# Three g tiles moved within the on-chip memory of a fused attention and two-MLP kernel

## The chip, the cores and the metric

The kernel runs on one core of a Trainium2 chip. The metric is the device time in microseconds (us) of one execution. Before the change three executions took 1518.82, 1520.11 and 1520.95 us; the median is 1520.11 us.

## The reference

Three stages follow each other. `attention`: q, k and v have 8 batches, 8 heads, 576 positions and 64 columns each; every block of 64 positions attends to itself alone (scores times 1/8, softmax, times v). Its result, seen as x of 4608 tokens by 512, goes through two MLPs:

```python
h = x @ w_in                                   # 512 -> 2048
g = np.maximum(h, 0.0) + np.log1p(np.exp(-np.abs(h)))
x = g @ w_out                                  # 2048 -> 512
h = np.maximum(np.maximum(x @ w1, x @ w2), x @ w3)   # 512 -> 768
out = h @ w_out2                               # 768 -> 512
```

The inputs come as float64 and are rebuilt as pairs of float32 numbers on the chip; all results are float32.

## The kernel before

**Tiling.** Tokens are cut into nine blocks of 512 (b), the hidden width of the first MLP into sixteen strips of 128 (j). Each operand of a matrix product is a tile of 128 partitions by 2 by 512 numbers in float32r: the first half holds the rounded values, the second what rounding left. A product is made in three passes (line 26, `PASS`): high times high, high times low, low times high. So each matmul of TensorE has a moving operand of 512 (or 256) columns, and a stationary operand of 128 columns that a weight load brings in before it. One matmul, one weight load.

**The lines.** `mlp1` holds the first MLP. Line 746 is its first product: 12 matmuls per block and strip, weights and x both in slots, into a `ph` bank. ScalarE takes softplus out of it (line 756), `cut_up` splits the result into a g tile (line 252 writes the high half, line 259 the low half), and line 766 is the second product: 12 matmuls, in which the g tile is the moving operand and a slot holds the weights. In the second MLP line 916 makes the products (moving 256 columns, all operands in slots). `mlp2_out`, line 1034, makes the last product, in which the g tile is the stationary operand and a slot is the moving one. Lines 670 and 723 are the two products of the attention of later blocks, each a batch of 12 and 24 matmuls (moving 256 and 128 columns, all in slots). Line 723 takes its weights 64 columns at a time and its moving operand in pieces of 32 numbers (128 bytes) that lie apart.

**The order.** Each step is an operation with a cost and a due time in a plan (`Plan.order`, lines 102 to 175); the plan simulates the engines with these costs, picks the order and hands out the places. It sees names and counts of places and no address. So two layouts with the same lists of places give the same instructions on every engine, in the same order, with the same waits.

**The layout.** A tile gets its address when it is first made: tiles stand in the order in which they are made, each rounded up to 32 bytes per partition. A partition holds 229,376 bytes; the last slot ends at 229,152. The first tiles are `ident`, `drop` (the offset column, 4 bytes), `mx` (four tiles of 32 bytes for maxima and sums), `rq` (2048 bytes), then the three g tiles (4096 bytes each), nine `tmp`, `rk`, `rv`, `p`, and behind them 46 slots of 4096 bytes (`s` in the profile). A slot takes weights, x, loaded pieces or parts of q, k and v in turn. 4096 and 2048 are multiples of 512, so in the kernel before rq, g, tmp and every slot start at 288 over a multiple of 512 bytes. Every operand of lines 746, 766, 916, 1034 and 670 starts at a multiple of 512 bytes from the start of its tile, so it too starts at 288.

Of the kernel before, what the change touches and what calls it, by code (L numbers as in the profile page):

```python
# [10 lines left out]
F32 = mybir.dt.float32  # L11
F32R = mybir.dt.float32r
# [8 lines left out]
P = 128  # L21
# [157 lines left out]
def tile_kernel(ctx: ExitStack, tc: tile.TileContext, q, k, v, w_in, w_out, w1, w2, w3, wo2, out):  # L179
    nc = tc.nc  # L180
    B, H, S, D = q.shape
# [8 lines left out]
    TB = 512  # L190
# [5 lines left out]
    pool = ctx.enter_context(tc.tile_pool(name="sb", bufs=1))  # L196
# [5 lines left out]
    def mem(kind, n, shape, dt, where=pool):  # L202
        return [where.tile(shape, dt, name=f"{kind}{i}") for i in range(n)]

    ident = pool.tile([P, P], F32, name="ident")
    drop = pool.tile([P, 1], F32, name="drop")
    small = {"mx": mem("mx", 4, [P, H], F32), "rq": mem("rq", 1, [P, TB], F32)}

    places = {

# [5 lines left out]
        "load": list(range(3)),  # L216
        "load0": list(range(4)),
        "pair": list(range(2)),
        "g": mem("g", 3, [P, 2, TB], F32R),
        "tmp": mem("tmp", 9, [P, TB], F32),  # L220
        "rk": mem("rk", 1, [P, TB], F32),
        "rv": mem("rv", 1, [P, TB], F32),
# [943 lines left out]
```

## Time and profile before

| | us |
|---|---|
| median of three executions | 1520.11 |
| the profiled execution | 1520.93 |
| its span, first to last instruction | 1519.1 |
| TensorE busy (PE) | 1499.5 |
| weight loads busy (PEld) | 1317.1 |
| VectorE busy (DVE) | 968.2 |
| ScalarE busy (ACT) | 592.5 |

The profiled execution took 1.8 us more than its span. In the profile PE is a matmul and PEld the weight load that may run beside one. Busy time of a group of matmuls counts each to its modelled end, past the start of the next; the distance from the first start of one batch to that of the next is the measure of what a batch takes. `g<-tmp,g` reads: written tile, arrow, read tiles.

### The profile page before, as it was taken

Reading aid. Unit: us, or ns where it says so; the run is one execution under the profiler, and the core shown is the slowest. Engines: PE = TensorE matmul, PEld = TensorE weight load, DVE = VectorE, ACT = ScalarE, POOL = GpSimd, SP = SyncE. Lnnn points to the kernel's source line nnn. Section 1 sums busy time; section 2 is a strip of 40 time slices with the busy share of each in tenths; the row PEclk is TensorE's granted clock in tenths of the full one; section 3 lists DMA queues with packets and bytes.
Section 4 is the critical chain, followed back from the end, with each engine's and each line's share of the span. In section 5 each row is a group of like instructions: output and inputs, shape, how many; then the busy total and the mean of one; then the engine's idle time right before and its main releaser. Section 6 shows DMA issues by size and latency. Waiting matters only on the chain.

```text
span 1519.1 us, 23062 instructions
## 1 busy us (share of the span) xinstructions
PE 1499.5 (99%) x8930; PEld 1317.1 (87%) x8930; DVE 968.2 (64%) x1841; ACT 592.5 (39%) x1123; POOL 4.6 (0%) x11
## 2 busy tenths in 40 slices
PE   6999999999999999999999999999999999999998
PEld 5787888888888888888888888999999999999997
DVE  7988877867776767767677465554544535445443
ACT  5754344443444343443343344432322323223221
POOL 0000000000000000000000000000000000000000
PEclk9999999999999999999999999999999999999999
DMA  9354233543434325244342221222322222222222
GB/s 257 118 141 129 63 89 98 148 113 77 139 90 109 98 58 146 70 101 101 77 120 81 71 92 54 78 70 84 112 69 85 84 77 105 84 84 76 78 70 84
DMA packets 235214, 147.29 MB, mean 97 GB/s; under 512 B 167008, under 2 KB 202848, under 8 KB 235104
## 3 DMA queue, kind: packets, MB, share of 16 engines
q1 hardware_dynamic: 231904, 144.24, 33.2%
q10 hardware_dynamic: 3200, 1.57, 0.5%
q8 instruction: 70, 1.15, 0.3%
q14 instruction: 40, 0.33, 0.1%
HBM read 109.58 MB, written 36.18 MB: 96 GB/s over the span
## 4 chain that ended last, share of the span: by engine, by line
PE 97%; ACT 1%; DMA 1%; DVE 0%; issue 0%; ACTq 0%
PE acc L766 26%; PE ph L746 26%; PE ph L916 15%; PE one L916 12%; PE acc L1034 10%; PE aps L723 3%; PE aps L670 3%; PE acc L609 1%; PE ph L372 1%; PE acc L560 1%; ACT s L252 1%; DMA s<-in_v_dram 1%; PE acc L529 0%; PE ph L371 0%; DMA s<-wo2d 0%
## 5 line engine op out<-in xcount | busy, mean ns | idle before, releaser
L746 PE MATMUL ph<-s,s 128*128 128x512 f32 x1728 | 416.5, 390 | 1.2 <-DVE s L259 0.9
L766 PE MATMUL acc<-g,s 128*128 128x512 f32 x1728 | 415.3, 390 | 0.0
L766 PEld LDWEIGHTS acc<-g,s 128*128 128x128 f32 x1728 | 322.9, 188 | 67.2 <-issue 1.0
L746 PEld LDWEIGHTS ph<-s,s 128*128 128x128 f32 x1728 | 321.5, 188 | 67.8 <-DVE s L259 1.2
L916 PE MATMUL ph<-s,s 128*128 128x256 f32 x1944 | 267.8, 283 | 0.0
L259 DVE TENSOR_TENSOR tmp<-one,tmp 128x256 f32<-128x256 f32 x241 | 101.9, 423 | 246.9 <-PE one L916 213.1
L916 PEld LDWEIGHTS ph<-s,s 128*128 128x128 f32 x1944 | 251.8, 192 | 4.1
L252 ACT COPY tmp<-ph 128x256 f32<-128x256 f32 x268 | 100.0, 373 | 347.7 <-PE ph L916 346.5
L259 DVE TENSOR_TENSOR g<-tmp,g 128x512 fp32r<-128x512 f32 x198 | 136.2, 688 | 146.3 <-ACT g L252 145.5
L756 ACT ACTIVATE tmp<-ph 128x512 f32<-128x512 f32 x144 | 86.2, 598 | 305.4 <-PE ph L746 302.7
L916 PE MATMUL one<-s,s 128*128 128x256 f32 x1458 | 201.6, 283 | 0.0
L916 PEld LDWEIGHTS one<-s,s 128*128 128x128 f32 x1458 | 186.7, 192 | 0.2
L259 DVE TENSOR_TENSOR s<-tmp,s 64x512 fp32r<-64x512 f32 (+1 forms) x212 | 142.3, 675 | 24.9 <-ACT s L252 21.0
L1034 PE MATMUL acc<-s,g 128*128 128x512 f32 x648 | 157.1, 391 | 0.5 <-DMA s<-wo2d 0.5
L252 ACT CAST s<-tmp 128x512 fp32r<-128x512 f32 (+2 forms) x190 | 115.2, 610 | 60.4 <-DVE tmp L641 26.6
L1034 PEld LDWEIGHTS acc<-s,g 128*128 128x128 f32 x648 | 118.3, 188 | 23.3 <-DMA s<-wo2d 0.9
L252 ACT CAST g<-tmp 128x512 fp32r<-128x512 f32 x192 | 119.4, 622 | 25.6 <-PE acc L766 16.4
L259 DVE TENSOR_TENSOR tmp<-tmp,tmp 128x256 f32<-128x256 f32 (+1 forms) x152 | 83.0, 547 | 3.9
L252 ACT COPY p<-aps 64x512 f32<-64x512 f32 x50 | 29.1, 583 | 66.9 <-PE aps L670 65.7
L252 ACT COPY tmp<-acc 128x512 f32<-128x512 f32 (+1 forms) x66 | 37.3, 588 | 33.4 <-PE acc L1034 15.8
L723 PEld LDWEIGHTS aps<-s,s 128*64 128x64 f32 x672 | 44.5, 135 | 3.7 <-DVE s L259 0.2
L670 PEld LDWEIGHTS aps<-s,s 128*128 128x128 f32 x336 | 44.0, 191 | 2.2
(97 smaller groups left out, 953.8 us busy)
## 6 DMA issues: line engine op xcount, KB each, us to landing
s<-wo2d SPq DMA_DIRECT2D x54, 512.0 KB, 3.3
s<-in_moe_w_out_dram SPq DMA_DIRECT2D x22, 512.0 KB, 4.8
x2d<-tmp SPq DMA_DIRECT2D x36, 256.0 KB, 2.9
s<-in_moe_w_dram SPq DMA_DIRECT2D x18, 512.0 KB, 4.1
s<-x2d SPq DMA_DIRECT2D x18, 512.0 KB, 4.6
s<-in_moe_w_in_dram SPq DMA_DIRECT2D x16, 512.0 KB, 4.9
out_dram<-tmp SPq DMA_DIRECT2D x29, 256.0 KB, 4.5
pd<-tmp SPq DMA_DIRECT2D x28, 256.0 KB, 2.2
```

Of the source, the lines that this page charges most:

```text
L252: nc.scalar.copy(dst(), src())
L259: return op({"D": 0.69 * n}, lambda e: nc.vector.tensor_tensor(dst(), a(), b(), f), r=r, w=w, **kw)
L372: nc.tensor.matmul(o, ident, a.t, start=False, stop=False)
L560: nc.tensor.matmul(o[:, h], qT()[:, h * P:(h + 1) * P], blk[0]()[:, 2 * h:2 * h + 2].rearrange("p u e s -> p (u e s)"), start=True, stop=True,
L609: nc.tensor.matmul(o[:CH, c], rv()[:, c * CH:(c + 1) * CH], blk[1]()[:, c].rearrange("p e s -> p (e s)"), start=True, stop=True,)
L670: nc.tensor.matmul(o[:, h], Qh.t[:, l, h * P:(h + 1) * P], kb[m].t[:, 2 * h * P:2 * (h + 1) * P], start=(n == 0), stop=(n == 2),)
L723: nc.tensor.matmul(o[:CH, c], Vh.t[:, l, c * CH:(c + 1) * CH], z[m][:, c % 2, c // 4, c // 2 % 2], start=(n == 0), stop=(n == 2),)
L746: nc.tensor.matmul(ph.t, w[:, wi, kk * P:(kk + 1) * P], x[kk].t[:, xi], start=(kk == 0 and wi == 0 and xi == 0), stop=(kk == KD - 1 and wi ...
L756: in_line("y", op({"A": 0.6}, lambda e: nc.scalar.activation(l.t, ph.t, AF.Softplus), r=[ph], w=[l], alloc=[l]))
L766: nc.tensor.matmul(acc[m // 2].t[:, m % 2], w[:, wi, m * P:(m + 1) * P], g.t[:, gi, :], start=(first and wi == 0 and gi == 0), stop=(last ...
L916: nc.tensor.matmul(dst(), ws.t[:, wi, col + kk * P:col + (kk + 1) * P], x.t[:, xi, kk * HT:(kk + 1) * HT], start=(first and kk == 0 and wi ...
L1034: nc.tensor.matmul(acc[t // 2].t[:, t % 2], g.t[:, gi, t * P:(t + 1) * P], wo.t[:, wi], start=(j == 0 and wi == 0 and gi == 0), stop=(j == ...
```

## The change

The order in which the small tiles are made is another one. `rq` and the first g tile are made ahead of `mx`, `drop` stands between the second and the third g tile, and two new tiles that nothing reads or writes (32 and 64 bytes) stand ahead of and behind the third g tile. The lists that the plan gets have the same length and order. The addresses, in bytes from the start of a partition:

| tile | before | by 512 | after | by 512 | by 64 (before, after) | slots minus tile, by 512, after |
|---|---|---|---|---|---|---|
| rq | 1824 | 288 | 1664 | 128 | 32, 0 | 256 |
| first g | 3872 | 288 | 3712 | 128 | 32, 0 | 256 |
| second g | 7968 | 288 | 7936 | 256 | 32, 0 | 128 |
| third g | 12064 | 288 | 12096 | 320 | 32, 0 | 64 |
| first tmp | 16160 | 288 | 16256 | 384 | 32, 0 | 0 |
| first slot | 40736 | 288 | 40832 | 384 | 32, 0 | 0 |

Before, the last column is 0 for all. Counted the other way, tile minus slots, the three g tiles are at 256, 384 and 448. The last slot ends at 229,248.

```diff
     ident = pool.tile([P, P], F32, name="ident")
+    small = {"rq": mem("rq", 1, [P, TB], F32), "g": mem("g", 1, [P, 2, TB], F32R)}
+    small["mx"] = mem("mx", 4, [P, H], F32)
+    small["g"].append(pool.tile([P, 2, TB], F32R, name="g1"))
     drop = pool.tile([P, 1], F32, name="drop")
-    small = {"mx": mem("mx", 4, [P, H], F32), "rq": mem("rq", 1, [P, TB], F32)}
+    pool.tile([P, 8], F32, name="apart0")
+    small["g"].append(pool.tile([P, 2, TB], F32R, name="g2"))
+    pool.tile([P, 16], F32, name="apart1")
...
         "pair": list(range(2)),
-        "g": mem("g", 3, [P, 2, TB], F32R),
         "tmp": mem("tmp", 9, [P, TB], F32),
```

## Rows read from the trace of the kernel before

**Rows 1.** The page: busy time, share of the span, instructions; granted clock by slices.
```profile
span 1519.1 us, 23062 instructions
...
PE 1499.5 (99%) x8930; PEld 1317.1 (87%) x8930; DVE 968.2 (64%) x1841; ACT 592.5 (39%) x1123; POOL 4.6 (0%) x11
...
PEclk9999999999999999999999999999999999999999
```

**Rows 2.** The page: the chain that ended last, shares by engine.
```profile
PE 97%; ACT 1%; DMA 1%; DVE 0%; issue 0%; ACTq 0%
```

**Rows 3.** Busy time by stretch, then granted clock, DMA share, GB/s.
```profile
400.00:935.00 535.00, 535.00 (x2790) 450.55 (x2790) 361.77 (x640) 217.54 (x370) 0.00 (x0) 1.00 0.35 92
935.00:1300.00 365.00, 365.00 (x2609) 345.39 (x2608) 185.29 (x386) 116.77 (x273) 0.00 (x0) 1.00 0.25 83
```

**Rows 4.** Groups by line and shape, TensorE: count | busy, mean ns | idle before.
```profile
L746 PE MATMUL ph<-s,s 128*128 128x512 f32 x1728 | 416.5, 390 | 1.2 <-DVE s L259 0.9 <-ACT s L252 0.3
L766 PE MATMUL acc<-g,s 128*128 128x512 f32 x1728 | 415.3, 390 | 0.0
L916 PE MATMUL ph<-s,s 128*128 128x256 f32 x1944 | 267.8, 283 | 0.0
L916 PE MATMUL one<-s,s 128*128 128x256 f32 x1458 | 201.6, 283 | 0.0
L1034 PE MATMUL acc<-s,g 128*128 128x512 f32 x648 | 157.1, 391 | 0.5 <-DMA s<-wo2d 0.5
```

**Rows 5.** Order of time on TensorE, 318 to 343 us: start, length, batch.
```profile
317.98 1.60 PE L723 MATMUL aps<-s,s 128*64 128x128 f32 x24
319.42 2.96 PE L766 MATMUL acc<-g,s 128*128 128x512 f32 x12
322.22 2.88 PE L746 MATMUL ph<-s,s 128*128 128x512 f32 x12
324.94 2.88 PE L766 MATMUL acc<-g,s 128*128 128x512 f32 x12
327.66 2.88 PE L746 MATMUL ph<-s,s 128*128 128x512 f32 x12
...
338.54 1.59 PE L670 MATMUL aps<-s,s 128*128 128x256 f32 x12
339.97 2.91 PE L746 MATMUL ph<-s,s 128*128 128x512 f32 x12
342.71 1.60 PE L723 MATMUL aps<-s,s 128*64 128x128 f32 x24
```

**Rows 6.** Order of time on TensorE, 1297 to 1305 us.
```profile
1297.37 2.91 PE L1034 MATMUL acc<-s,g 128*128 128x512 f32 x12
1300.11 0.88 PE L916 MATMUL ph<-s,s 128*128 128x256 f32 x6
...
1301.55 1.60 PE L916 MATMUL ph<-s,s 128*128 128x256 f32 x12
1302.99 1.60 PE L916 MATMUL one<-s,s 128*128 128x256 f32 x12
```

**Rows 7.** Groups by line and shape, weight loads: count | busy, mean ns.
```profile
L766 PEld LDWEIGHTS acc<-g,s 128*128 128x128 f32 x1728 | 322.9, 188 | 67.2 <-issue 1.0
L723 PEld LDWEIGHTS aps<-s,s 128*64 128x64 f32 x672 | 44.5, 135 | 3.7 <-DVE s L259 0.2
```

**Rows 8.** Groups by line and shape, TensorE, at 278.3 us: one matmul.
```profile
L746 PE MATMUL ph<-s,s 128*128 128x512 f32 x1 | 0.4, 388 | 0.0
```

**Rows 9.** Order of time, weight loads, the one that followed it.
```profile
278.73 0.19 PEld L746 LDWEIGHTS ph<-s,s 128*128 128x128 f32 x1 [0.73 <-ACT s L252]
```

**Rows 10.** Groups by line and shape, VectorE: two operations on 128 by 512.
```profile
L259 DVE TENSOR_TENSOR g<-tmp,g 128x512 fp32r<-128x512 f32 x198 | 136.2, 688 | 146.3 <-ACT g L252 145.5
L259 DVE TENSOR_TENSOR p<-p,mx 128x512 f32<-128x512 f32 x56 | 38.6, 689 | 1.2
```

**Rows 11.** Longest pieces of the chain that ended last: start, length.
```profile
2.34 8.62 DMA s<-in_v_dram
```

## The prediction

> **What bounds the kernel now.** I read the busy shares first: TensorE is busy for 1499.5 of 1519.1 us, at a granted clock of 0.9 or more of full speed in every slice [rows 1]. The chain of waits says the same from its end: 97% of it is TensorE [rows 2]. Then the stretches: from 400 to 1300 us TensorE is busy for every one of the 900 us at a clock of 1.00 (its 2.4 GHz level), while VectorE is busy for 547 and ScalarE for 334 of them [rows 3]. So the time is what the matmuls take one after the other, and the question is what one matmul takes.
>
> A group's mean (390 ns) is no answer, since matmuls overlap. The distance from one batch's start to the next is. A batch of 12 of line 766 takes 327.66 - 324.94 = 2.72 us, one of line 746 takes 324.94 - 322.22 = 2.72 us [rows 5]: 226.7 ns for each matmul of 512 columns, whether its moving operand is a g tile or a slot. With 256 columns 12 take 302.99 - 301.55 = 1.44 us, 120 ns each [rows 6]. The 24 of line 723, with 128 columns and half the weights, take 319.42 - 317.98 = 1.44 us, 60 ns each [rows 5]. Two lengths give the rate: (226.7 - 120) / 256 = 0.417 ns a column, one cycle of the 2.4 GHz level. So 512 columns account for 213.3 ns, and 13.3 ns are over; at 256 columns 13.3 again; at line 723 6.7. This excess is the only thing that the placing of operands could touch in the steady state. For the matmuls that read a g tile, 1728 of line 766 and 648 of line 1034 [rows 4], it comes to 2376 x 13.3 ns = 31.6 us.
>
> **The change part by part.**
>
> *Order and waits.* Nothing is added, removed or moved: the plan never sees an address, and its lists of places are the same. Cost 0, and I see no reason for another value.
>
> *Distance between g and the slots.* All operands of lines 766 and 1034 now start 0 apart by 512 bytes; after, 64, 128 or 256. Two bounds. If all of the excess is the two reads of TensorE meeting in the memory, and apart they never do, 31.6 us go. If a start apart makes them meet where they don't now, the nearest row is the batch of line 766 behind line 723, which takes 322.22 - 319.42 = 2.80 us instead of 2.72 [rows 5]: 6.7 ns for each of its 12, and 2376 x 6.7 = 15.8 us more. I take 0, for three reasons.
> First, the reads don't keep their distance. A load of 128 columns lasts 188 ns and one of 64 lasts 135 [rows 7]: 53 / 64 = 0.83 ns a column, half the rate of the moving operand. While a load passes its 512 bytes (106 ns), the moving operand passes 240 to 255 columns, 960 to 1020 bytes. The distance slides by 450 to 510 bytes in every load. Whatever distance is bad, nearly all of them come up already, from any start.
> Second, line 723 is a sample of other starts. Its weights start at 0 or 256, its moving pieces at 0 or 128, and of its 24 matmuls six start at each of the four combinations; only six start 0 apart. If a start of 0 cost 6.7 ns and others nothing, the batch would take 24 x 53.3 + 6 x 6.7 = 1.32 us. It takes 1.44 [rows 5].
> Third, a matmul at 278.3 us had no load beside it (the next one came after 0.73 us of idle time) [rows 9] and lasted 388 ns [rows 8], against a mean of 390 in its line [rows 4]. Its end is modelled, so this is weak; as far as it goes the load costs the moving operand 2 ns, not 13.3.
>
> The Trainium skill, "TensorE: Matmul & The Clock Gate", section "Wait — 56ns, not 53.3ns?", has warm matmuls start N / 2.4 GHz + about 2.5 ns apart, 215.7 ns at 512 columns; this trace has 226.7 and differs. By that rule 11 ns of the excess are something particular to this kernel, and if they are the equal starts, an estimate from the page is 2376 x 11 = 26.1 us less, 1494.8; by the rows alone the change gives 0.
>
> *Alignment of everything.* The pads also shift tmp and all slots by 96 bytes: from 32 over a multiple of 64 to a multiple of 128. That touches every matmul of lines 746, 766, 916 and 1034, also those that read no g tile. No row shows another alignment. The upper end of a gain is the excess as a whole at 512 columns: 4104 x 13.3 = 54.6 us; a loss can't be excluded, and 1 ns for each of the 7506 would be 7.5 us. I take 0: over the lines of the trace the excess follows the number of weights, 13.3 for 128 and 6.7 for 64, and that is the same after.
>
> *VectorE and ScalarE.* The subtraction that writes the g tiles reads both inputs 0 apart by 512 bytes and takes 688 ns; the one of the maxima from p, with inputs 128 bytes apart (160 against 288), takes 689 [rows 10]. So VectorE doesn't care, cost 0; ScalarE, for which no row shows another distance, I take the same way. Were it 50 ns either way on both, TensorE's work would cover it: in the whole run it waits 0.9 us for VectorE and 0.3 for ScalarE at line 746, and for neither at line 766 [rows 4].
>
> *DMA into slots.* Only the first loads stand on the chain: 8.62 us for v [rows 11]. Its pieces of 256 bytes touch five stretches of 64 bytes from an unaligned start and four from an aligned one. If that is what it costs, a fifth goes, 1.7 us; as much the other way is the bound of a loss. I take 0.
>
> *Sum.* 1520.93 us of the profiled execution + 0 = 1520.93. It stands 0.8 us above the median of the three executions (1520.11), within their spread, and I name the median: **1520.1 us**.
>
> **The rivals.**
>
> *The equal starts are the excess (faster).* Lines 766 and 1034 fall from 226.7 to 213.3 ns at best: 1520.9 - 31.6 = 1489.3 us. For it: the excess is there in every batch, all of whose operands start equal. Against it: the slide of the distance, line 723, and the matmul without a load.
>
> *The alignment pays (faster).* 2048 bytes from an address 32 above a multiple of 128 touch 17 stretches of 128 bytes, from a multiple 16; with 256 columns 9 and 8. If the excess is paid by stretch, one of 17 at 512 columns is 0.78 ns, times 4104 matmuls 3.2 us; one of 9 at 256 columns is 1.5 ns, times 3402 another 5.0 us. (The third g tile is not at a multiple of 128; that takes 0.4 us off.) The time is between 1512 and 1517 us, middle 1514. For it: 7506 matmuls are touched, so 0.4 ns each is already 3 us. Against it: the excess halves with the weights, which stretches of the moving operand alone don't explain at 256 columns.
> A rule of the Trainium skill speaks against this one: "SBUF — State Buffer", section "Specifications (TRN2)", has lines of 16 bytes; 32 and 0 over a multiple of 64 are both whole lines, and by it nothing is spared. No row here shows it.
>
> *Each change of distance upsets the stream (slower).* Place: the switches between lines 746 and 766. Today both run at the same distance, and a switch costs nothing: 2.72 us follow 2.72. Where the stream changes its length, the next batch pays: line 746 behind line 670 takes 342.71 - 339.97 = 2.74 us [rows 5], line 1034 behind line 916 takes 1300.11 - 1297.37 = 2.74 [rows 6], and line 766 behind line 723 2.80. So two streams of TensorE that are in step need some matmuls to find it again. If a jump of the distance by 64 to 256 bytes throws them out of step, all 144 batches of line 766 pay on the way in and the next batch on the way out: 288 x 0.02 us = 5.8 us, 1526 us; at 0.08 us each, 1543. It decides from 10 ns a switch (288 x 10.5 ns = 3.0 us). For it: something there has to fall into step. Against it: moving operand and weights jump by multiples of 512 bytes in every batch with no trace of it, and the pieces of line 723 jump by other amounts at 60 ns a matmul.
>
> **How the numbers follow.** A measurement of this kernel tells about 0.2%, 3.0 us, from no change. No change (1518 to 1522.5): 0.57. Equal starts were the excess (about 1489): 0.08. Alignment (1512 to 1517, more if the stretches are others): 0.17. Out of step (1526, up to 1543): 0.18. So faster 0.25, same 0.57, slower 0.18. The range reaches down over the alignment's prices to 1510, and up past the lower price of the switches to 1531; outside lie the 0.08 at 1489, some of the alignment's large end and a third of the slower case, together less than 0.2.
>
> **What would show it.** Right: batches of lines 766 and 746 still follow at 2.72 us, line 916 at 1.44 us for 12, line 1034 behind line 916 at 2.74. Equal starts as the cause: line 766 nearer to 2.6 us with line 746 at 2.72. Alignment: line 746, which reads no g tile, moves too, and line 916 below 1.44. Out of step: line 746 behind line 766 at 2.74 or more. The forecast is wrong if any of these four distances moves by over 0.01 us; if they stay and the time moves, the cause is in the first 60 us or at the end, where TensorE waits.

## The result and the profile after

Four runs of the changed kernel took 1527.13 to 1529.55 us, median 1528.72; four of the kernel before 1518.82 to 1521.02, median 1520.53. The ratio is 1.0052 [1.004, 1.0064]: about 8.2 us more. The prediction said 1520.1 and no change. The change made the kernel slower, and the prediction's term for it was wrong.

The page of the profiled execution (1528.32 us) answers to [rows 1]:

```profile
span 1526.5 us, 23062 instructions
...
PE 1506.2 (99%) x8930; PEld 1314.4 (86%) x8930; DVE 967.9 (63%) x1841; ACT 592.2 (39%) x1123; POOL 4.6 (0%) x11
...
PEclk9999999999999999999999999999999999999999
```

The instructions are as many as before, the other engines are as busy, and the granted clock is 0.9 or more of full speed in every slice. Only TensorE is busy longer, by 6.7 us. The groups by line and shape say where (count, then busy us and mean ns of one, then idle time before). The change adds four lines to the file, so 770 is the 766 of [rows 4], 750 the 746, 920 the 916, 1038 the 1034, 727 and 674 the 723 and 670:

```profile
L770 PE MATMUL acc<-g,s 128*128 128x512 f32 x1728 | 422.1, 393 | 0.0
L750 PE MATMUL ph<-s,s 128*128 128x512 f32 x1728 | 417.7, 391 | 1.2 <-DVE s L263 0.9 <-ACT s L256 0.3
L920 PE MATMUL ph<-s,s 128*128 128x256 f32 x1944 | 267.8, 283 | 0.0
L920 PE MATMUL one<-s,s 128*128 128x256 f32 x1458 | 201.6, 283 | 0.0
L1038 PE MATMUL acc<-s,g 128*128 128x512 f32 x648 | 157.9, 393 | 0.4 <-DMA s<-wo2d 0.4
```

The line that reads the g tiles as moving operand gained 6.8 us, line 750 behind it 1.2, line 1038, which reads them as weights, 0.8. Line 920, which touches no g tile, is the same to the last digit. The waits of line 750 are the same too: no engine holds TensorE up any longer than before.

The order of time on TensorE (start, length, batch) shows what a batch takes, as [rows 5 and 6] did:

```profile
318.63 1.60 PE L727 MATMUL aps<-s,s 128*64 128x128 f32 x24
320.07 3.00 PE L770 MATMUL acc<-g,s 128*128 128x512 f32 x12
322.91 2.90 PE L750 MATMUL ph<-s,s 128*128 128x512 f32 x12
325.64 2.96 PE L770 MATMUL acc<-g,s 128*128 128x512 f32 x12
328.44 2.90 PE L750 MATMUL ph<-s,s 128*128 128x512 f32 x12
331.18 2.88 PE L770 MATMUL acc<-g,s 128*128 128x512 f32 x12
333.90 2.88 PE L750 MATMUL ph<-s,s 128*128 128x512 f32 x12
336.62 2.95 PE L770 MATMUL acc<-g,s 128*128 128x512 f32 x12
339.41 1.58 PE L674 MATMUL aps<-s,s 128*128 128x256 f32 x12
...
1296.61 2.94 PE L1038 MATMUL acc<-s,g 128*128 128x512 f32 x12
1299.39 0.88 PE L920 MATMUL ph<-s,s 128*128 128x256 f32 x6
```

The four batches of line 770 read the second, third, first and second g tile. From start to start they take 2.84 (behind line 727, where it was 2.80), 328.44 - 325.64 = 2.80, 2.72 and 2.79 us. Before, a batch behind line 746 took 2.72 whichever tile it read. So the first tile, 256 bytes off, costs nothing; the second, 128 off, 0.07 us a batch; the third, 64 off, 0.08. The batch of line 750 behind the third takes 331.18 - 328.44 = 2.74, behind the first 2.72.

The distances from one matmul's start to the next, summed by line over the whole trace, make the account: line 770 took 6.9 us more than 766, 750 took 1.2 more, 1038 0.8; line 613, in the first 60 us, took 1.5 less than 609; the other lines moved by 0.1 together. That is 7.5 us; the span grew by 1526.5 - 1519.1 = 7.4.

VectorE didn't care, as said; the group that answers to the first row of [rows 10]:

```profile
L263 DVE TENSOR_TENSOR g<-tmp,g 128x512 fp32r<-128x512 f32 x198 | 136.1, 688 | 152.9 <-ACT g L256 152.0
```

### The profile page after: what moved, and what is told of

Read it like the earlier page. It is cut to its first block, busy times and chain, and to the rows that moved or that the text cites. A ratio compares the mean times of both kernels' runs of the same rounds, so it can differ in the third digit from the quotient of the medians.

```text
span 1526.5 us, 23062 instructions
## 1 busy us (share of the span) xinstructions
PE 1506.2 (99%) x8930; PEld 1314.4 (86%) x8930; DVE 967.9 (63%) x1841; ACT 592.2 (39%) x1123; POOL 4.6 (0%) x11
## 4 chain that ended last, share of the span: by engine, by line
PE 97%; DVE 2%; DMA 1%; ACT 0%; issue 0%; ACTq 0%
PE acc L770 26%; PE ph L750 26%; PE ph L920 15%; PE one L920 11%; PE acc L1038 10%; PE aps L727 3%; PE aps L674 3%; DMA s<-in_q_dram 1%; PE acc L564 1%; PE acc L613 1%; PE ph L376 1%; PE acc L533 0%; ACT s L256 0%; DVE s L263 0%; DVE tmp L263 0%; DMA s<-wo2d 0%
## 5 line engine op out<-in xcount | busy, mean ns | idle before, releaser
L770 PE MATMUL acc<-g,s 128*128 128x512 f32 x1728 | 422.1, 393 | 0.0
L263 DVE TENSOR_TENSOR s<-tmp,s 64x512 fp32r<-64x512 f32 (+1 forms) x212 | 142.2, 674 | 25.4 <-ACT s L256 21.3
```

The costliest lines, as they stand in the source:

```text
L263: return op({"D": 0.69 * n}, lambda e: nc.vector.tensor_tensor(dst(), a(), b(), f), r=r, w=w, **kw)
L770: nc.tensor.matmul(acc[m // 2].t[:, m % 2], w[:, wi, m * P:(m + 1) * P], g.t[:, gi, :], start=(first and wi == 0 and gi == 0), stop=(last ...
```

## The experiments

From here on *distance* is the start of the moving operand minus the start of the weights, by 256 bytes. In the changed kernel it is 0, 128 and 192 for line 770 with the first, second and third g tile, and 0, 128 and 64 for line 1038. *Price* is the time from one matmul's start to the next, a batch divided by 12: 226.7 ns for 2.72 us, 229 for 2.75, 232.5 for 2.79, 233.3 for 2.80.

The theories at the start: the distance between the two operands of one matmul sets its price (D); a change of distance between two batches throws the streams out of step (S, the prediction's slower rival); the g tile's own start sets it (P). All kernels are the one before with its small tiles made in another order; the fences show the tiles as they are then made (a number behind a pad is its bytes), and lines that are changed elsewhere. Not shown in them: the setting `dynamic_dma_scratch_size` is 512 instead of 1024 in every kernel but three (all tiles at 256, all tiles 64 below, the changed alignment). Batches at distance 0 take 2.72 us with either value. A kernel for which no ratio is given was executed once.

**All starts equal, at a multiple of 512.** This moves all g tiles and slots together from 288 over a multiple of 512 bytes to 0.

```diff
-    ident, drop, mx, rq, ..., g0, g1, g2
+    ident, rq, mx, drop, pad 224, g0, g1, g2
```

> All three g tiles and all slots start at a multiple of 512 bytes; the distance between them is 0, as before the change. Theory D (what costs is the distance between the start of the moving operand and that of the weights): the same as before, 1520.5 us within 2, batches of the first MLP 2.72 us apart. Rival P (what costs is a tile's own start: in the changed kernel the second g tile stands at 0 over a multiple of 256 bytes and its batch takes 2.79 us): every batch with 512 columns takes 2.79, 1520.5 + (288 + 54) x 0.07 = 1544 us. Rival A (the alignment of slots to 64 or 128 bytes saves time that the g tiles' cost hid in the changed kernel): 1512 to 1517 us.

Measured: 1518.56 us, ratio 0.9983 [0.9974, 0.9992]. Batches take 2.72 us, and the busy time of all four lines is that of [rows 4]. For the second product:

```profile
L770 PE MATMUL acc<-g,s 128*128 128x512 f32 x1728 | 415.3, 390 | 0.0
```

So P falls. The 2.3 us that it gains are not in the steady state: from start to start, the sums of these four lines differ from those before by 0.1 us at most. The row of the first 60 us (length, then busy us of PE, PEld, DVE, ACT, POOL; granted clock, DMA share, GB/s) has a clock of 1.00 and 278 matmuls:

```profile
0.00:60.00 60.00, 47.43 (x278) 37.44 (x279) 52.47 (x105) 37.29 (x64) 0.74 (x7) 1.00 0.75 228
```

In the kernel before that stretch has:

```profile
0.00:60.00 60.00, 46.40 (x256) 37.58 (x257) 50.03 (x100) 35.39 (x60) 0.74 (x7) 0.94 0.83 228
```

The executions of the changed kernel and of others here show 0.91 to 0.97 there. Why the start-up got further in this one was not tried; the smaller setting alone doesn't do it, since kernels with 0.91 to 0.97 have it too.

**All three g tiles at 256.** All the jumps of 256 bytes between lines 750 and 770 are there, 144 times.

```diff
+    ident, rq, g0, g1, g2, mx, drop, pad 96
```

> All three g tiles 256 bytes from the slots by 512, slots and other tiles where the changed kernel has them. Theory D, with the first g tile's batches of the changed kernel (2.72 us) as its row: nothing is lost, 1520.5 us within 2. Rival S (each jump from one distance to another puts the two streams of TensorE out of step, whatever the distances): 288 switches, all batches of the second product 2.79 or more and the next ones 2.74, 1531 to 1535 us.

Measured: 1520.89 us, 0.9998 [0.9988, 1.0007]. Order of time on TensorE:

```profile
321.81 2.88 PE L750 MATMUL ph<-s,s 128*128 128x512 f32 x12
324.53 2.88 PE L770 MATMUL acc<-g,s 128*128 128x512 f32 x12
327.25 2.88 PE L750 MATMUL ph<-s,s 128*128 128x512 f32 x12
329.97 2.88 PE L770 MATMUL acc<-g,s 128*128 128x512 f32 x12
```

Each takes 2.72 us. A jump of 256 bytes costs nothing, so S, by which every jump costs, falls, and 256 bytes are as good as none.

**All three g tiles 64 below the slots.** The third tile's distance for all three.

```diff
+    ident, rq, mx, drop, pad 32, g0, g1, g2, pad 64
```

> All three g tiles 64 bytes below the slots by 512, as the third one in the changed kernel. Theory D: all 144 batches of the first MLP's second product take 2.80 instead of 2.72 us, and the first product's batch behind them 2.74: 1520.5 + 144 x 0.08 + 112 x 0.02 = 1534 us. Rival S: only a change between distances costs, and there are as many as in the all_256 kernel, so the same time as that one. Rival M (it is the mixture of three distances in one kernel): 1520.5 us.

Measured: 1533.44 us, 1.0081 [1.0066, 1.0096]. Its group of the second product, and then the order of time:

```profile
L771 PE MATMUL acc<-g,s 128*128 128x512 f32 x1728 | 425.9, 395 | 0.0
```

```profile
327.43 2.96 PE L771 MATMUL acc<-g,s 128*128 128x512 f32 x12
330.23 2.90 PE L751 MATMUL ph<-s,s 128*128 128x512 f32 x12
332.97 2.96 PE L771 MATMUL acc<-g,s 128*128 128x512 f32 x12
```

Every batch of line 771 takes 2.80 us, the one behind it 2.74. The price is paid by each of the 12 matmuls (in the records all of them start 233 ns apart); finding the step again costs the next batch 0.02. 12.6 us for three tiles at 192, against 8.2 for one at 128, one at 192 and one at 0.

**Ahead by 64, 128 and 192.** Two readings of D: the moving operand, twice as fast as the load, runs into its start from behind (then being ahead is free); or only the distance by 256 counts.

```diff
+    ident, rq, g0, pad 64, g1, pad 64, g2, mx, drop, pad 160
```

> The g tiles stand 64, 128 and 192 bytes above the slots by 512 (in the changed kernel 256, 128 and 64 below). Theory D1 (catching up: the moving operand, read at twice the rate, starts behind the weights and runs into them): a start ahead runs away from the weights, so all three tiles' batches take 2.72 us. Theory D2 (only the distance by 256 counts): 128 above equals 128 below, 2.79 us; 192 above equals 64 below, 2.80 us; 64 above equals 192 below and is new. Time by D1 1520.5, by D2 1527 to 1531 us.

Measured: 1532.43 us. Batches of line 772 with the g tile 128, then 192 and 64 ahead (the last line is cut off by the end of the window):

```profile
301.75 2.96 PE L772 MATMUL acc<-g,s 128*128 128x512 f32 x12
304.55 2.90 PE L752 MATMUL ph<-s,s 128*128 128x512 f32 x12
...
326.77 2.96 PE L772 MATMUL acc<-g,s 128*128 128x512 f32 x12
329.57 2.90 PE L752 MATMUL ph<-s,s 128*128 128x512 f32 x12
332.31 2.93 PE L772 MATMUL acc<-g,s 128*128 128x512 f32 x12
335.08 2.93 PE L752 MATMUL ph<-s,s 128*128 128x512 f32 x12
337.85 0.40 PE L772 MATMUL acc<-g,s 128*128 128x512 f32 x1
```

2.80 (2.79 in the records), 2.80 and 2.77 us (2.76): 192 ahead costs what 64 behind costs, 128 ahead what 128 behind costs. The distance by 256 decides; the reading with the runner from behind falls. With the tile 64 ahead its own batch costs less, but the batch of line 752 behind it takes 337.85 - 335.08 = 2.77 instead of 2.74. The two together lose about 0.09 us, much as at 128 and 192 (0.09 and 0.10). That is part of why the time came out above the 1527 to 1531 us expected.

**The x slots moved instead, by 128, 64 and 192.** If it is the distance of any two operands, a first product whose x slots stand apart from its weights must pay too. The slots are laid by hand, the weights first, then a pad, then the slots of x; g at 96, 160 and 224 (first kernel), at +16, -16 and -4 bytes (second), at 0 (third).

```diff
+    for i in [*range(32), 44, 45]:
+        pool.tile([P, 2, TB], F32R, tag=f"s{i}", name=f"s{i}_0")
+    pool.tile([P, 32], F32, name="between")      # 16: x64, 48: x192
+    for i in range(32, 44):
+        pool.tile([P, 2, TB], F32R, tag=f"s{i}", name=f"s{i}_0")
```

> The slots of x and of the attention's big tiles stand 128 bytes above those of the weights (by 256), and the g tiles 96, 160 and 224 above, so the first product of the first MLP and the products of the second MLP (256 columns) lose their equal starts too. Theory D (the distance by 256 of the moving start from the weights' start sets the price): the first product's batches take 2.79 us as the second's did at 128; the three new distances give three new prices between 2.72 and 2.80. On the 256 columns two theories part. D-narrow (their 120 ns hold a collision that equal starts make, since at 226.7 / 512 ns a column they would take 113.3): at 128 above 12 of them take another time than 1.44 us, down to 1.36. L (the load of 128 columns sets the 120 ns): 1.44 stays. Time by D and L 1533 to 1545 us, by D-narrow down to 1510.

> x slots 64 bytes above the weights' slots by 256; the g tiles 16 above, 16 below and 4 below. Theory D: the first product's batches take what the second's did at 64 above, 2.76 us; a start 4 or 16 bytes off 0 is new. If the price steps by 64-byte stretches (theory D-step) 16 above costs nothing and 4 and 16 below cost as 64 below, 2.80; if it grows with the distance (theory D-slope) 4 bytes cost next to nothing. 256 columns: theory L 1.44 us for 12, D-narrow another time. Time by D and L 1528 to 1537 us.

> x slots 192 bytes above the weights' slots by 256, g tiles at 0. Theory D: the first product's batches take 2.80 us, the second's 2.72 and some 0.02 more behind the first's, the last product (a slot moving, g as weights, both at 0) 2.75 behind the 256 columns: 1520.5 + 144 x 0.08 + 144 x 0.02 = 1535 us with 256 columns as they are (theory L); theory D-narrow another time than 1.44 us for 12 of them, worth up to 23 us either way.

Measured: 1540.68, 1526.31 and 1525.88 us. The first product, which before paid 226.7 ns, paid 233 at 128 and 192 and 229 at 64 (233 in 10 of its 87 batches behind the second product). So it is any two operands. The g tiles at 96, 160 and 224 took 2.79 to 2.82 us a batch, up to 0.02 more than expected. A g tile 4 or 16 bytes off cost 231 to 236 ns in the second product where I had expected a price in proportion or none below a step: both wrong. And the 256 columns of the second MLP, whose distance changed with x, became cheaper: by 2.3, 9.8 and 7.1 us in the three kernels, summed from start to start. That is why the second and third kernel came out below the times expected. At 192 (third kernel), where 12 had taken 1.44 us [rows 6]:

```profile
1281.61 1.58 PE L924 MATMUL ph<-s,s 128*128 128x256 f32 x12
1283.02 1.58 PE L924 MATMUL one<-s,s 128*128 128x256 f32 x12
...
1285.14 2.88 PE L1042 MATMUL acc<-s,g 128*128 128x512 f32 x12
1287.86 0.87 PE L924 MATMUL ph<-s,s 128*128 128x256 f32 x6
```

1.41 us for 12, 117.7 ns each. The last product, at distance 0 behind them, takes 2.72 and not the 2.74 of before. The second kernel's matmuls of 256 columns had two prices at one distance, 113.3 or 117.7 ns, whole runs of them at one or the other.

**The halves of g 64 apart.** Each g tile's low half stands 64 bytes above its high half. This tells whether a matmul pays for its own weights or for those that are loaded beside it for the next one. In the first kernel passes alternate; in the second the passes run in blocks of eight and four.

```diff
+    whole = pool.tile([P, 2 * (TB + 16)], F32R, name="g0")
+    small["g"].append(whole.rearrange("p (u n) -> p u n", u=2)[:, :, :TB])
```

```diff
-            for m in range(KD):
-                for wi, gi in PASS:
+            for wi, gi in ((0, 0), (1, 0), (0, 1)):
+                for m in range(KD):
...
-            for t in range(TB // P):
-                for gi, wi in PASS:
+            for gi, wi in PASS:
+                for t in range(TB // P):
```

> The high half of every g tile starts at 0 from the slots by 256, the low half 64 above. In the second product the moving operand goes high, high, low, in the last product the weights do, with the moving slot at 0. Which load does a matmul meet? Theory N (the next one's, which is read beside it): in the last product the second matmul of each three, whose successor has the low half as weights (moving 64 below them), is the long one. Theory O (its own weights): the third of each three is. By both a three of the last product takes about 3 x 226.7 + 6.7 ns and a batch 2.75 + 0.02 us; a batch of the second product, where every third moving operand is 64 above, 2.72 + 4 x 0.0023 = 2.73 us and up to 2.76. Time 1522 to 1527 us. Rival: a step off the period of the three upsets all of them, 1528 us and more.

> As the halves kernel, but the passes are taken in blocks: the second product uses the high half of g eight times and then the low half four times, and so does the last product with its weights. Long enough to settle. Theory D: the last four of a batch cost what their distance costs (second product 64 above: about 229 ns each, last product 64 below: 233.3), the first eight of the second product 226.7, so its batch takes 2.73 us and, with some matmuls to settle, up to 2.76, less than the 2.78 of the halves kernel. Which load is met: in the last product the eighth matmul has the low half next (theory N: it is long) but the high half as its own weights (theory O: it is not). Time 1524 to 1527 us.

Measured: 1530.2 and 1528.82 us. With alternating passes all twelve were upset (2.77 to 2.78 us a batch, as the rival there had it), and nothing could be told. In blocks the last product read its low half as weights in the ninth matmul for the first time. The groups of one matmul each, the eighth and then the ninth of a batch (its end is modelled):

```profile
L1042 PE MATMUL acc<-s,g 128*128 128x512 f32 x1 | 0.4, 388 | 0.0
...
L1042 PE MATMUL acc<-s,g 128*128 128x512 f32 x1 | 0.4, 398 | 0.0
```

The eighth, beside which the ninth's weights load (in the records that load starts 3 ns after the eighth matmul), has the undisturbed 388 ns; the ninth, whose own weights they are, 398. From start to start the medians are 226 and 236. This speaks for a matmul's own weights. A batch of the second product took 2.75 us, as expected; the time is above its range because each batch of the first product behind it took 2.745 us instead of 2.72.

**The x slots 64 up, g and the last product's slots at 0 or with them.** Since distance 64 made 256 columns cheaper, three kernels looked for the layout that keeps that and loses least at 512.

```diff
+    for i in range(32):                          # x64_g0, x64_g64: [*range(32), 44, 45]
+        pool.tile([P, 2, TB], F32R, tag=f"s{i}", name=f"s{i}_0")
+    pool.tile([P, 16], F32, name="between20")
+    for i in range(32, 46):                      # x64_g0, x64_g64: range(32, 44)
+        pool.tile([P, 2, TB], F32R, tag=f"s{i}", name=f"s{i}_0")
```

In the kernel with both g and x at 64 a pad of 192 bytes stands behind g2.

> Slots of x 64 bytes above those of the weights as in the x64 kernel, all g tiles at 0. Theory D with states (at 64 above, 256 columns run at 113.3 or at 117.7 ns, according to how the matmuls ahead of them ended): first product 2.75 us a batch, second 2.72 to 2.74, last product 2.72 to 2.75, 256 columns 1.36 or 1.41 us for 12. With 117.7: 1520.5 + 144 x (0.03 + 0.02) - 3402 x 0.0023 = 1520; with 113.3: 1520.5 + 7 - 3402 x 0.0067 = 1505 us. Theory L: 1.44, 1528.

> As x64_g0, but the slots that the last product moves stand 64 above too, so it moves 64 above its weights (g) and leaves the stream in another state: last product 2.75 us a batch. Theory D with states: 256 columns at 113.3 or 117.7 ns, 1505 or 1521 us; if the state does not hang on what ran ahead, the same as x64_g0.

> As x64_g0, but the g tiles stand 64 above the weights too, so the whole first MLP runs at one distance (64 above) and the last product at 64 below. Theory D with states: both products 2.75 us a batch without jumps, last product 2.80; 256 columns 113.3 or 117.7 ns: 1520.5 + 288 x 0.03 + 54 x 0.05 - 8 = 1524 us, or 1509 us with 113.3.

Measured: 1523.98, 1509.66 and 1522.27 us. The first missed both times named for it (1520 and 1505). In the first and the third, 256 columns cost 117.7 ns; in the second, in which slots 44 and 45 (moved in the last product) went up too, nearly all cost 113.3. So what a matmul of 256 columns pays at distance 64 hangs also on the last product between them: it stood at distance 0, 64 and 192 in the three. And a batch at distance 0 is not always free. In the first kernel, between batches at 64:

```profile
327.13 2.93 PE L774 MATMUL acc<-g,s 128*128 128x512 f32 x12
329.90 2.93 PE L754 MATMUL ph<-s,s 128*128 128x512 f32 x12
332.66 2.93 PE L774 MATMUL acc<-g,s 128*128 128x512 f32 x12
```

Line 774 takes 2.77 us at distance 0. In the records its matmuls are back at 227 ns from the eleventh on. So the steady price at 0 is the same, and finding the step again costs 0.05 us here, more than the 0.02 I had expected.

**The changed kernel's alignment at distance 0.** All starts at a multiple of 128, as the slots of the changed kernel have, and nothing apart.

```diff
+    ident, rq, mx, drop, pad 96, g0, g1, g2
```

> The part of the change that the g tiles have no share in: all slots and tmp stand where the changed kernel has them (128 over a multiple of 256), and the g tiles with them, at distance 0. Theory D alone: 1520.5 us within 1.5, batches of both products 2.72 us. Theory D with alignment (zero_512 ran 2.3 us below the kernel before, outside the batches): 1517.5 to 1519 us, the difference in the first 60 us.

Measured: 1519.74 us, 0.9993 [0.9984, 1.0002]; line 770 is busy for 415.4 us, and batches take 2.72 us:

```profile
323.40 2.88 PE L770 MATMUL acc<-g,s 128*128 128x512 f32 x12
326.12 2.88 PE L750 MATMUL ph<-s,s 128*128 128x512 f32 x12
328.84 2.88 PE L770 MATMUL acc<-g,s 128*128 128x512 f32 x12
```

So alignment is worth nothing that can be measured, and the whole price of the change is the distance.

**The best layout again, in five executions, and one more.** The second of the three above, and one in which the moved slots of the last product stand at 128 and its g tile at 64, so that its distance is 64 again.

> The kernel that ran at 1509.66 us in one look, timed. Theory D with states: 113.3 ns for nearly all products of 256 columns, so 1509.5 us within 1.5; ratio 0.9925.

> As x64_g0_wo64, but the g tiles stand 64 above the weights and the slots that the last product moves 64 above the g tiles. Theory D with states: the whole first MLP at one distance saves the jumps (batches of 2.75 instead of 2.76 and 2.77: 144 x 0.04 = 5.8 us at most, 2.7 by the rows of x64_g64), the last product is again 64 above its weights and leaves the state in which 256 columns run at 113.3 ns: 1507 us. Rival: the state is set by something other than the last product's distance; then 117.7 ns and 1521 us.

Measured: 1508.87 us, 0.9925 [0.9911, 0.9938], and 1520.41 us, 0.9997 [0.9989, 1.0006]. The first beats both kernels. Its groups of 256 columns, and then its order of time:

```profile
L924 PE MATMUL ph<-s,s 128*128 128x256 f32 x1944 | 255.6, 276 | 0.0
L924 PE MATMUL one<-s,s 128*128 128x256 f32 x1458 | 192.2, 276 | 0.0
```

```profile
1281.24 1.52 PE L924 MATMUL ph<-s,s 128*128 128x256 f32 x12
1282.60 1.52 PE L924 MATMUL one<-s,s 128*128 128x256 f32 x12
...
1284.64 2.91 PE L1042 MATMUL acc<-s,g 128*128 128x512 f32 x12
1287.38 0.84 PE L924 MATMUL ph<-s,s 128*128 128x256 f32 x6
```

1.36 us for 12 against 1.44. Summed from start to start, 256 columns give 21.3 us back, the two products of the first MLP cost 4.5 and 5.1 more. That leaves 11.7 of the 12.0 us measured. The two prices are no chance: of the 701 batches of the two MLPs, 698 took the same time within 2 ns in both profiled executions of this layout.

The other kernel missed (1507 expected). Its last product at distance 64:

```profile
1290.61 2.96 PE L1046 MATMUL acc<-s,g 128*128 128x512 f32 x12
1293.41 0.87 PE L928 MATMUL ph<-s,s 128*128 128x256 f32 x6
```

2.80 us instead of the 2.74 of the layout above, and the matmuls of 256 columns went from 113.3 to 117.7 ns behind the first batch of line 1046. So distance 64 has two states, 229 and 233 ns. In the good layout neither operand's start (by 256) changes on the way into the last product; here both move by 64. What sets the state stays open.

## Why the prediction was wrong, point by point

*Order and waits, 0:* right. The count of instructions, the waits of TensorE and the other engines' times are the same.

*Distance between g and the slots:* this is the step that failed. "I take 0, for three reasons" should have been about 9: line 770 paid 6.9 us, the batches behind it 1.2, line 1038 0.8. It is a term that was mis-sized, and a price of the right size stood in the prediction as the upper end: 6.7 ns a matmul. That is the price of line 770 at 192 (233.3 against 226.7), and about that at 128 (232.7), for two of three tiles; the first tile, at 256, is free. Line 1038 paid only 1.3 ns a matmul.

That the upper end's 6.7 ns fit is luck. The row that it came from, line 766 behind line 723, is no price of each of 12 matmuls: in the records the first of them takes 281 ns and those from the seventh on 227. It is a cost of the change of length. Of the three reasons:

- *The distance slides through all values in every load, so no start is special.* The slide may be there, but the conclusion doesn't follow: moving the start of a g tile by 64 or 128 bytes moved the price of line 770 by 6 to 7 ns (all at 192: every batch 2.80 us), and by 256 not at all.
- *Line 723 is a sample of other starts.* It is a sample of another shape. At 256 columns distances of 64 and 192 lower the price (120 to 117.7 or 113.3), at 512 they raise it. So a batch of short matmuls says nothing of long ones. By 256 bytes its four combinations are also only two distances, 0 and 128.
- *The matmul without a load lasts as long as one with it.* True, and consistent with a price of 0 at distance 0, the only distance that the trace of before had at 512 columns. It said nothing of another.

*Alignment, 0:* right; with the starts equal the changed alignment gave 0.9993 [0.9984, 1.0002].

*VectorE, ScalarE and the loads, 0:* right for VectorE (688 ns) and ScalarE (592.2 us); for the loads nothing shows beyond the 1.5 us by which the start-up moved, which may be any run's.

*The rivals.* "Out of step" had the right place, the right sign and 1526 us, near the 1528.7 measured, but the wrong mechanism: its price per switch would have shown with all tiles at 256, where nothing was paid. Only the 1.2 us in the batches behind, 0.015 to 0.02 each, are of its kind. So it was luck, too, that the range of 1510 to 1531 held the time measured: it reached up that far for this rival's sake. "The equal starts are the excess" is wrong where it was put, at 512 columns; for the 256 columns, for which it made no forecast, it holds in part: 6.7 of their 13.3 ns went in the best layout. The rule weighed with it (the Trainium skill, "TensorE: Matmul & The Clock Gate", section "Wait — 56ns, not 53.3ns?"), 215.7 ns at 512 columns, was seen in no layout: the lowest steady price in any of these traces is 226.7.

Of the four distances that the prediction named as checks, three moved by more than 0.01 us: line 750 behind the third g tile to 2.74, line 770 from 2.72 to 2.79 and 2.80 for two tiles of three, and line 1038 behind line 920 from 2.74 to 2.78.

What is shown: the distance alone makes the change's price, and 0 and 256 are alike. What is supported by one kernel only: that a matmul pays for its own weights. What stays open: why a distance costs (that the two reads meet in the memory is one guess, which no run here tests), and what picks between two prices at one distance.

## What to carry to other kernels

When TensorE is the bound and every matmul brings its own weights, the place of a tile in memory can be part of the matmul's price: measure it from batch start to batch start, by which tile is read. A trace in which all operands start alike holds no evidence on other distances, so the cost of leaving that point has to be bounded by the largest row near it and not taken as nothing because an argument on rates says so. A layout that is best for one length of matmul can be wrong for another: here the gain lay at 256 columns.

## What the runs showed of the hardware

- Steady price of a matmul of 512 columns by distance (start of moving operand minus start of weights, by 256 bytes): 226.7 ns at 0; 229 or 233 at 64; 231 to 233 at 128; 233.3 at 192; in the second product 231 to 236 at 4 or 16 bytes off.
- Of 256 columns: 120 ns at 0; 113.3 or 117.7 at 64; 118 to 120 at 128; 117.7 at 192.
- A batch of 512 columns at 0 takes, in most cases, 0.015 to 0.02 us more behind one at 128 or 192 and settles in about six matmuls; behind one at 64 it takes 0.05 more and settles in about ten. A jump of 256 costs nothing.
- One distance can have two prices that last for whole runs of matmuls, by what ran ahead; a second execution shows the same ones.
